# A residual block of a diffusion network on one core: every engine's instruction order written anew

## The chip, the cores and the metric

The kernel runs on one core of one Trainium2 chip, alone. The metric is the device time of one execution in microseconds, as the median of several runs. A profiled execution has a time of its own, and its span (from the first to the last recorded instruction) is a little shorter than that time.

## What is computed

The reference is the residual block of a diffusion UNet: group norm and SiLU, a 3x3 convolution, an embedding added per channel, group norm and SiLU again, a second 3x3 convolution, and the input added. B is 2, there are 512 channels, images of 64 x 64, four groups, and an embedding of 1152 numbers; everything is bfloat16 in and out.

```python
def gn(z, gamma, beta):                       # 4 groups of 128 channels
    mu = zr.mean(-1); var = ((zr - mu) ** 2).mean(-1)
    return (zr - mu) / jnp.sqrt(var + 1e-5) * gamma + beta
h = conv3(_silu(gn(x, g1, be1)), w1)          # 3x3, padding 1
h = h + (_silu(t_emb) @ w_emb).reshape(B, C, 1, 1)
h = conv3(_silu(gn(h, g2, be2)), w2)
return x + h
```

## The kernel before

**Tiling.** The channels are four tiles of 128, `ct` on the input side and `ot` on the output side. A *chunk* is 32 rows of one image (`b`, `ch`), so each of the two layers has four chunks, and each chunk four *groups*, one for each `ot`. A group is written here as layer.chunk.ot (g0.3.2 is the first layer's last chunk, third output tile). The convolution is done on rows in Winograd's way: each four rows of output come from six transformed planes `pos` 0 to 5. Planes 1 and 2 (in some chunks 1 to 4) are transformed along the columns too and called nested.

**The work of a chunk.** `produce_V` makes the transformed activations V of one chunk, tile by tile: SP loads the rows (line 619), ACT applies scale, bias and SiLU (`activate`, L626), and `transform` makes the planes on DVE (a scaled copy at line 641, then L642, L649, L662 to L679, then the columns at L557 and L562). Line 611 and 613 are POOL's memsets of the padding rows. Two V buffers stand in turn. `prep_U` makes the transformed weights U of half a tile (`pr`): loads of R and `g1t` by SP (the latter at line 404), scaled copies (lines 422 to 426), a sum by a DMA that accumulates, issued by POOL (L431), the combinations on DVE (L420), and `nest_U` (L393) for the nested planes. In layer 0, U of the later tiles is made during the first groups; U1.0p0 means layer 1, tile 0, first half. There are three `stage` buffers for the loads.

**The work of a group.** PE multiplies: nested planes with 256 columns (tile `nst`, L943), the others with 512 (tiles `mid` and `acc`, L935). PSUM has three buffers of two banks (`nst`, `mid` and an `aux` for sums) and two of one bank (`acc`). ACT copies the results out (`evac`, L306), DVE combines columns (`cols_mid`, L988 to L990, tiles `tu` and `rm`) and rows (`rows_z`, L1002 to L1009), and the two `acc` tiles of planes 0 and 5 are copied out in `close_group` while the next group is already under way. A POOL DMA adds z to y (L1070), SP stores to `h_scr` (L1074), and ACT takes the sums for the next norm (`sum_up`, L796). `tu` and `rm` have one buffer each.

**The norms.** `gn_scale_bias` takes the sums over the partitions by a matmul (L317) and then, on DVE, the negative variance (L319 to L330). POOL raises it to the power -1/2, for one column (L332) or four (L337), and DVE makes the scale `sc_all` (L333 or L338) and the bias `nb_all` from it. The first image's norm of layer 0 is done tile by tile (four powers of one column); the second image's, gn1, and the two of layer 1, gn2, in one power each.

**Who does a copy.** All scaled copies go through `scaled_copy`, which counts them; character k of the string `FLIP` moves copy k from its engine of default (DVE for `times`, ACT for `evac`) to the other. A copy on DVE is line L307, one on ACT L306.

**What sets the order.** `ORDER` is a table for each of five engine queues (PE, DVE, Activation, Pool, SP): the instructions of that engine by their number as written, in the order in which they are to be issued. `in_order` chains each to the one ahead of it:

```python
for a, z in zip(ranks, ranks[1:]):
    tc.add_manual_dep(mine[z], mine[a].name, info, reason="order")
```

The dependency only sets the order and adds no semaphore. The tables cover 3239 instructions of PE, 853 of DVE, 367 of ACT, 115 of POOL and 103 of SP. Waits between engines follow from the data and the buffers, as always. A planner has worked out the tables and the string from estimated durations of each kind of instruction and delays between engines.

Of the kernel before, what the change touches and what calls it, by code (L numbers as in the profile page):

```python
# [18 lines left out]
class _Background:  # L19
# [45 lines left out]
0-22 90-121 23-43 122 44-53 123-124 156-157 125-135 158-160 136-153 161-187 154-155 54-78 188-252 254-255 79-89 253  # L65
256-270 320-335 271-285 318 286-298 336-351 299-317 370-401 352 358 353 359-360 408-409 319 410 364 361-363 411-413
420 365 354-355 366-367 356-357 402-407 421-435 368-369 414-417 436-437 418-419 438-451 470-485 461 458-460 462
452-453 463 486-501 464-469 454-457 511-512 508-510 502-503 513-514 504-505 515 506-507 516 520-521 517-519 522-532
544 533-534 545 535 546-548 536 549-551 537 552-557 592 558-566 568-569 580 570 581 571-573 582-583 574 567 538-543
593 575-579 594-598 584-591 599-614 624-630 615-623 631-646 648 647 673-693 649-659 705 661-664 660 665 706 666-672  # L70
707-721 737-741 722-726 749 694-704 742-743 750 727-728 751-754 729-736 761-762 777 744-748 778 755-760 763 793-801
779 802-816 780-792 825-831 837-840 764-776 841-848 832-836 817-824 849-854 865-866 855-856 867-869 857 870-879 881
880 882-893 913 894-898 858-864 899-901 925-927 902-904 914-923 928-930 905 931 906-912 937-938 932-933 939-952 924
953 934-936 954-955 969-970 956-958 971 993 959-962 972-973 963-968 974-979 1001 994 980-985 1025-1026 986-992
1013-1014 1027-1028 1002-1003 1015 995-1000 1029-1032 1016-1022 1033 1023-1024 1041 1057 1004 1042-1043 1034-1040
1044 1005-1007 1058-1064 1008-1009 1045-1048 1081 1010-1012 1082 1065-1066 1083 1067-1070 1085-1086 1084 1049-1056
1097-1098 1071-1080 1099-1100 1109 1101-1102 1110 1103-1108 1087-1091 1111-1124 1092-1096 1125 1141 1126-1129 1142
1130-1140 1143-1147 1157-1172 1148-1156 1173-1178 1185-1190 1179-1180 1191-1192 1181 1193 1182 1194-1196 1183-1184
1197 1213-1214 1198-1200 1215-1216 1201-1204 1217-1219 1205-1212 1220-1232 1245-1260 1233-1244 1261-1262 1273-1274
1263-1271 1275-1281 1272 1282-1288 1301 1289 1302-1307 1290-1300 1308-1321 1333-1345 1322-1323 1346-1348 1324-1331  # L80
1349-1352 1332 1353 1361 1373-1375 1389-1390 1376-1378 1391-1394 1379-1386 1354 1395-1400 1355-1356 1387-1388
1401-1402 1362 1403-1405 1357 1363-1370 1358 1371 1359 1372 1360 1406-1412 1421 1413 1422-1427 1437 1428-1430 1438
1431-1435 1414-1416 1436 1417 1439 1418-1420 1450 1440-1442 1451-1452 1443-1446 1462 1447-1449 1453-1461 1478-1484
1463-1469 1494 1485-1490 1470-1473 1495 1491-1493 1496-1497 1474-1477 1498-1508 1526-1530 1510-1523 1509 1524-1525
1538-1542 1531-1535 1550 1566-1567 1536-1537 1543 1568 1544 1569-1570 1551-1554 1545-1548 1555-1557 1571 1558 1549
1559 1572-1580 1560-1565 1581-1597 1614-1616 1626 1617-1618 1627-1636 1598-1609 1637-1639 1610-1613 1640-1645
1619-1625 1646-1656 1670 1657 1671-1672 1658 1673-1679 1659-1661 1680-1685 1662-1669 1686-1698 1726-1730 1699-1701
1731 1702-1706 1714 1707-1710 1715-1725 1711 1732 1712-1713 1733-1740 1742-1743 1741 1758-1759 1744 1760 1745-1749
1761 1750-1757 1762-1773 1790-1793 1802 1774-1785 1794 1786-1789 1795 1803-1804 1796 1805-1806 1797-1798 1814
1807-1810 1799 1811-1813 1800-1801 1830-1837 1846-1847 1838-1839 1848-1854 1840-1843 1855-1857 1844-1845 1815-1818  # L90
1858-1859 1819 1860-1869 1820-1829 1870-1873 1882-1888 1894-1898 1889 1899-1900 1890-1893 1910 1901-1908 1874 1911
1926-1927 1909 1912 1928 1913-1916 1929 1875 1917-1922 1876 1923 1877 1924 1930-1931 1925 1878-1879 1932 1880-1881
1933-1949 1974-1979 1950 1980 1951-1955 1990-1992 1956-1957 1962 1958-1961 1963-1973 2006-2009 1981 2010-2015 1982
1993 2016-2018 1994-2003 2019-2021 2030 2022 2042-2043 2004-2005 1983-1987 2023-2028 2044 2031-2032 2029 2045-2048
1988-1989 2049 2033-2034 2050-2052 2054 2070 2086-2089 2055 2035 2090 2036 2071-2072 2037-2038 2053 2091 2056-2065
2092-2093 2066-2067 2039 2094 2068 2073 2040 2074 2095 2069 2075 2096 2041 2097-2102 2110 2103-2104 2111 2105-2108
2112 2123 2076 2124 2077-2080 2125 2081-2085 2126-2127 2113-2114 2128 2115-2117 2109 2118-2120 2129 2121-2122
2130-2131 2135-2143 2151 2144 2152-2153 2132-2133 2145-2146 2167 2147 2134 2154-2157 2148-2150 2158-2166 2168-2171
2183 2172-2182 2184-2197 2223-2224 2198 2225-2238 2199-2200 2211-2212 2201-2202 2239 2213 2240 2203 2255 2204-2205
2256-2257 2206-2209 2258-2260 2210 2214-2218 2241 2219 2242 2220-2222 2243-2250 2261-2262 2287 2251-2254 2263-2265  # L100
2299 2288-2293 2266-2269 2294-2295 2270-2285 2311-2314 2296 2286 2297-2298 2315-2325 2327-2331 2326 2332-2338
2343-2347 2339 2348-2349 2340 2350 2341-2342 2351-2358 2300-2310 2359-2367 2375 2368-2374 2376-2380 2399-2401 2387
2381 2402-2405 2382-2384 2406 2385 2388-2392 2415-2420 2393-2396 2421 2386 2422-2423 2407-2414 2424 2397 2425-2429
2431 2398 2430 2432-2438 2463-2465 2439-2462 2466-2468 2475-2476 2487 2477-2480 2488 2481-2482 2489 2483-2486 2503
2469-2474 2519-2534 2504-2508 2490-2502 2509-2518 2551-2556 2535-2550 2563 2557-2559 2564 2575 2565-2566 2576-2578
2567 2560-2561 2591 2568-2569 2579-2580 2592-2593 2581-2582 2607 2594 2608 2583 2609 2595 2584-2585 2596 2610-2613
2597-2601 2562 2614 2602 2615 2603-2604 2616 2605-2606 2617-2622 2570-2574 2586-2590 2639-2648 2651-2652 2649
2623-2638 2653-2656 2663-2671 2679 2672 2657 2673-2674 2650 2675-2677 2658 2678 2695-2705 2680-2694 2659-2662
2706-2726 2751-2756 2727-2728 2757-2758 2729-2731 2759 2739-2745 2760-2761 2746-2747 2762-2766 2748-2749 2767-2769
2750 2770-2773 2732-2734 2774-2781 2735-2738 2782-2793 2799-2811 2815-2820 2827-2829 2812-2814 2794-2798 2830-2831  # L110
2821-2822 2832-2834 2839 2823-2826 2835-2838 2840-2841 2855-2859 2842 2860-2862 2843 2863 2844-2854 2864-2866 2871
2867-2870 2872-2898 2935 2903-2905 2899-2902 2936-2949 2906-2910 2950 2911-2913 2951-2955 2919 2956-2962 2920 2963
2921 2967-2968 2922 2914-2918 2923 2969 2924-2925 2970-2971 2926 2964-2965 2972-2975 2966 2976-2978 2927 2979
2928-2929 2980-2982 2930-2931 2983-2985 2999-3000 2932-2934 3001-3005 2986-2998 3007 3006 3008-3014 3031-3039 3047
3040 3048 3041-3045 3049-3051 3046 3052-3055 3063-3064 3056-3057 3065 3058-3061 3015-3030 3066-3067 3062 3068-3069
3079 3070-3071 3080-3088 3072 3089-3093 3073 3094 3074-3075 3095 3159 3167 3096 3076-3078 3160 3097 3168 3161 3169
3162 3170-3173 3163-3166 3174 3098 3111-3112 3099-3104 3127 3113 3175 3183-3184 3114 3128 3115-3117 3129 3118-3119
3130 3105-3110 3131 3120-3123 3185-3186 3132 3124-3126 3187-3189 3133 3190 3143-3158 3134-3142 3176-3182 3191-3194
3215-3221 3195-3201 3222-3225 3202-3214 3226-3238""",
# [3 lines left out]
99 108 110 68 76 109 69 91 70 100 123 78 83 88 119 89 84 93 101 117 75 96 116 77 97 94 98 95 122 115 133 114 102 121  # L123
103 124 120 104 136 105 111 106 112 107 125 142 135 134 128 126 143 127 130 137 131 138 132 139 141 140 129 145 144
# [61 lines left out]
def kernel(  # L186
# [115 lines left out]
    def scaled_copy(o, i, f, on_act):  # L302
        k = n_copies[0]
        n_copies[0] += 1
        if on_act != (FLIP[k:k + 1] == "1"):
            return nc.scalar.activation(out=o, in_=i, func=ACT.Copy, scale=f)  # L306
# [921 lines left out]
```

## Time and profile before

| | before |
|---|---|
| runs (us) | 459.91, 460.68, 461.85 |
| median (us) | 460.68 |
| profiled execution: its time (us) | 461.23 |
| its span (us) | 459.1 |
| outside the span (us) | 2.1 |
| mean granted TensorE clock | 0.995 |
| PE, DVE, ACT, POOL busy (us) | 443.0, 435.6, 375.1, 76.4 |

A busy time counts each instruction from its start to its end; as consecutive ones overlap a little in the pipelines, the time from start to start is shorter. The first matmul starts at 1.4 us and the last ends at 453.6. In the table of slices the granted clock is below 9 tenths in one slice, around 234 us.

### The profile page before, as it was taken

How to read it: one execution, taken by the hardware profiler on the slowest of the kernel's cores; microseconds unless marked ns; L12 is line 12 of the kernel's file. 1: busy time of each engine (PE TensorE's matmuls, PEld its weight loads, DVE VectorE, ACT ScalarE, POOL GpSimd, SP SyncE). 2: the span in 40 equal slices, each digit the busy share in tenths (PEclk: the TensorE clock that was granted, in tenths of full speed). 3: DMA queues.
4: the chain of work that ended last, by engine and by line, in shares of the span. 5: the costliest groups of instructions: out<-in, count | busy, mean ns of one | idle time of the engine just before them, and what ended most of it. 6: DMA issues, size and time to landing. Idle time of an engine off the chain costs nothing.

```text
span 459.1 us, 8457 instructions
## 1 busy us (share of the span) xinstructions
PE 443.0 (96%) x3246; PEld 290.3 (63%) x3246; DVE 435.6 (95%) x857; ACT 375.1 (82%) x405; POOL 76.4 (17%) x119
## 2 busy tenths in 40 slices
PE   8988999999999999998989999999999999999995
PEld 7944455555555677666656555557676667668884
DVE  2999999989999999999999999999999899999986
ACT  5899997968967899889989999648686775869972
POOL 1231200041000000110211211124212121212110
PEclk9999999999999999999989999999999999999999
DMA  8998755544765463446889796375858769456673
GB/s 309 357 380 202 190 137 135 165 131 130 183 153 157 95 178 92 129 110 208 171 243 241 192 233 140 94 178 119 199 154 195 175 158 213 98 132 138 130 197 134
DMA packets 25010, 80.04 MB, mean 174 GB/s; under 512 B 2827, under 2 KB 6027, under 8 KB 24587
## 3 DMA queue, kind: packets, MB, share of 16 engines
q0 software_dynamic: 10080, 34.87, 37.2%
q1 hardware_dynamic: 14832, 44.64, 29.2%
q8 instruction: 25, 0.41, 0.3%
q14 instruction: 14, 0.11, 0.1%
q10 hardware_dynamic: 59, 0.01, 0.0%
HBM read 42.54 MB, written 16.78 MB: 129 GB/s over the span
## 4 chain that ended last, share of the span: by engine, by line
PE 48%; DVE 37%; issue 6%; ACT 4%; DMA 2%; POOL 2%; DVEq 0%; ACTq 0%; POOLq 0%
PE nst L943 22%; PE acc L935 18%; PE mid L935 6%; DVE V L679 4%; DVE ak L642 3%; DVE U L420 3%; DVE V L562 3%; DVE V L557 3%; DVE rm L990 2%; DVE U L393 2%; DVE ak L307 2%; DVE ak L649 2%; DVE V L669 1%; DVE tu L988 1%; DMA ak<-h_scr 1%
## 5 line engine op out<-in xcount | busy, mean ns | idle before, releaser
L943 PE MATMUL nst<-V,U 128*128 128x256 f16 x1600 | 205.3, 273 | 3.2 <-ACT rm L306 2.7
L943 PEld LDWEIGHTS <-U 128*128 128x128 f16 x1600 | 154.4, 97 | 50.3 <-issue 4.3
L935 PE MATMUL acc<-V,R 128*128 128x512 f16 x672 | 172.3, 384 | 3.1 <-ACT ring L306 1.7
L306 ACT ACTIVATE rm<-nst 128x1024 f16<-128x1024 f32 x98 | 98.1, 1024 | 23.4 <-PE nst L943 10.9
L935 PEld LDWEIGHTS <-R 128*128 128x128 bf16 x720 | 69.7, 97 | 68.4 <-issue 4.7
L935 PE MATMUL mid<-V,U 128*128 128x512 f16 x336 | 84.7, 384 | 1.6 <-DVE me L375 1.0
L626 ACT ACTIVATE ak<-ak,nb_all,sc_all 128x2112 f16<-128x2112 f16 (+1 forms) x28 | 59.8, 2148 | 4.6 <-DVE nb_all L525 1.9
L796 ACT ACTIVATE ring<-ring 128x2048 f16<-128x2048 f16 x32 | 61.3, 1914 | 1.4 <-ACT rm L306 0.7
L935 PEld LDWEIGHTS <-U 128*128 128x128 f16 x336 | 32.1, 97 | 36.1 <-ACT s_sb L450 1.1
L1070 POOL DMA_DIRECT2D ring<-ring x28 | 24.4, 872 | 148.0 <-ACT ring L306 131.4
L306 ACT ACTIVATE ring<-ring 128x512 f16<-128x512 f16 x47 | 27.8, 623 | 18.8 <-DVE ring L1002 10.5
L642 DVE TENSOR_TENSOR ak<-ak 128x2080 f16<-128x2080 f16 x32 | 40.0, 1249 | 0.8 <-ACT ak L306 0.6
L306 ACT ACTIVATE ak<-ak 128x520 f16<-128x520 f16 (+1 forms) x26 | 32.1, 1239 | 8.9 <-DVE ak L649 5.6
L679 DVE TENSOR_TENSOR V<-ak 128x1040 f16<-128x1040 f16 x54 | 39.0, 724 | 0.0
L562 DVE TENSOR_TENSOR V<-V 128x512 f16<-128x512 f16 (+1 forms) x62 | 35.2, 576 | 0.5 <-PE acc L935 0.5
L990 DVE TENSOR_TENSOR rm<-tu,rm 128x1024 f16<-128x1024 f16 x50 | 34.9, 698 | 0.9 <-DVE tu L988 0.5
L306 ACT ACTIVATE ring<-acc 128x512 f16<-128x512 f32 x55 | 31.3, 594 | 4.0 <-DVE ring L1009 3.1
L557 DVE TENSOR_TENSOR V<-V 128x1024 f16<-128x1024 f16 (+1 forms) x31 | 30.8, 996 | 0.0
L420 DVE TENSOR_TENSOR U<-U,g1t 128x1536 f16<-128x1536 f16 x32 | 30.6, 963 | 0.0
L989 DVE TENSOR_TENSOR tu<-rm 128x512 f16<-128x512 f16 x50 | 21.5, 431 | 1.6 <-ACT rm L306 1.6
L649 DVE TENSOR_TENSOR ak<-ak 128x1040 f16<-128x1040 f16 x32 | 23.0, 718 | 0.1
L669 DVE TENSOR_TENSOR V<-ak 128x1040 f16<-128x1040 f16 x32 | 22.9, 717 | 0.0
(131 smaller groups left out, 468.5 us busy)
## 6 DMA issues: line engine op xcount, KB each, us to landing
ring<-ring POOLq DMA_DIRECT2D x28, 512.0 KB, 4.7
ak<-h_scr SPq DMA_DIRECT2D x16, 528.0 KB, 5.4
h_scr<-ring SPq DMA_DIRECT2D x16, 512.0 KB, 3.7
ring<-in_x_dram POOLq DMA_DIRECT2D x14, 512.0 KB, 5.6
out_dram<-ring POOLq DMA_DIRECT2D x14, 512.0 KB, 5.2
ak<-in_x_dram SPq DMA_DIRECT2D x12, 528.0 KB, 4.9
R<-in_w_dram SPq DMA_DIRECT2D x16, 384.0 KB, 5.5
U<-U POOLq DMA_DIRECT2D x14, 384.0 KB, 5.3
```

Source lines behind the costliest of these rows:

```text
L306: return nc.scalar.activation(out=o, in_=i, func=ACT.Copy, scale=f)
L420: nc.vector.tensor_tensor(out=o, in0=i0, in1=i1, op=op)
L557: nc.vector.tensor_tensor(out=lo2.rearrange("p c q (t w) -> p (q t) c w", w=HALF), in0=plane_pair(0, HALF + 2), in1=plane_pair(1, HALF), o ...
L562: nc.vector.tensor_tensor(out=hi2[:, c].rearrange("p q (t w) -> p (q t) w", w=HALF), in0=i0, in1=i1, op=op)
L626: nc.scalar.activation(out=at[:, lo - r0:hi - r0, 1:W + 1], in_=sap, func=ACT.Silu, bias=nb_all[:, layer, b, ct:ct + 1], scale=sc_all[:, l ...
L642: nc.vector.tensor_tensor(out=diff, in0=diff, in1=below, op=ALU.add)
L649: nc.vector.tensor_tensor(out=rows(1, 2), in0=rows(1, 2), in1=rows(3, 2), op=ALU.subtract)
L679: nc.vector.tensor_tensor(out=o, in0=in0, in1=in1, op=op)
L796: behind(nc.scalar.activation(out=junk, in_=y, func=func, scale=scale, accum_out=acc), inst)
L935: nc.tensor.matmul(out, lhsT=w_direct(pos, ct, kx), rhs=rhs, start=first, stop=last)
L943: nc.tensor.matmul(accs["nst", (pos - 1) // 2][bank][:, q, :, plane, :], lhsT=lhsT, rhs=rhs.rearrange("p (t w) -> p t w", w=HALF), start=s ...
L990: nc.vector.tensor_tensor(out=msl[:, 1 - k:4 - k:2].rearrange("p q t w -> p q (t w)"), in0=tu[:].rearrange("p q t e w -> p q (t e w)"), in ...
```

## The change

All five tables of `ORDER` and the string `FLIP` are replaced; nothing else. The computation, the tiles, the buffers, the matmuls and the transfers are the same 4677 instructions in the tables. As told with the change, the new order was planned with longer times for GpSimd's powers (L332, L337) and for the weights' sums by transfers (L431), and with redrawn delays.

Of the 412 scaled copies 90 change engine: 50 go from DVE to ACT and 40 from ACT to DVE, so that DVE has 843 instructions and ACT 377. As an instruction's number in its table counts only the instructions of its engine, the numbers of DVE's and ACT's tables before and after don't denote the same instructions; PE's, POOL's and SP's do. Cut to the start of DVE's table, the small tables of POOL and SP, and the string:

```diff
@@ -62,110 +62,109 @@
 ORDER = {
...
     "DVE": """
-0 2 1 3-4 13-14 5 7 6 48 8 16 9 15 10 17 11 19 12 18 24-25 21 26 20 27 22 28 23 29-32 45 33 46 49 52 47 53 72 34 56
-35 50 38 54 71 36 55 37 39 57 51 40 58 41 74 113 42 73 80 85 43 81 44 87 86 79 59 82 60 92 61 90 62-64 66 65 118 67
...
     "Pool": """
-0 4 1 10-11 5 2-3 6-7 12-13 8-9 15 14 21-22 18 16-17 19 24 20 25 23 28 27 30 26 29 32-33 31 37 34 39 35 40 36 42 38
-41 47 43-45 49 46 50 48 64 52-53 65 55 51 56 54 68 57 69 59 58 60 62 61 63 66 81 67 70-73 78 74 83 75-77 86 79-80 82
-91 84-85 95 87-90 92 99 93 102 94 96-98 100-101 103-114""",
+0 4 1 10 5 11 2-3 6-7 12-13 8-9 21 14-15 22 16-17 20 18-19 25 24 23 28 27 30 26 29 32-33 31 37 34 39 35 40 36 42 38
+41 47 43 45 44 49 46 50 52 48 64 53 65 51 56 55 54 68 57 69 58-59 62 61 60 63 66 81 67 70-72 78 73-76 83 77 86 79-80
+82 91 84-85 95 87-90 92 99 93 102 94 96-98 100-101 103-114""",
     "SP": """
-0-13 17 19 21 18 20 23 14-15 22 16 25 28 30 33 24 26 29 31 27 32 37 35-36 34 39 38 40 42 44 43 41 45 48 50 47 46 49
-51 54 68 71 73 56 52 57 53 59 55 61 58 63 60 62 65 67 66 70 64 72 75 86-87 76-78 80 69 81-82 74 84 83 85 79 88-102""",
+0-13 17-19 21 23 20 14 22 15-16 25 28 30 33 24 26 29 31 27 32 37 35-36 34 39 38 40 42 44 43 41 45 48 50 46 49 47 54
+51 68 71 56 73 52 57 53 59 55 61 58 63 60 67 62 65 70 66 64 76 72 86 75 87 78 77 69 80 82 74 84 81 83 79 85 88-100
+102 101""",
 }
...
@@ -224,7 +223,7 @@
-    FLIP = "001011001000001100000000010000111000000010001111011111110000000001010001011000000001000000000001000000000000000000000000001000000000000000000000001101100000000000000000001000000010011110000000000001000000000000000001010000100000101001010001000010110111100100001101111100000111000000110010000100011001100000001110000001100000000010001001000011000000110011100000011111000000110000011000011100001100001110000111"
+    FLIP = "000110000000010000010000101000010101001110001001011111010000000011111000001111100001111100000100111001000000000101100000000001000001000000000000000101101000000010000000001010000000001011001000000001000000100000000010000101001000111001110010000011010111110100001101101100000011010000110110000110011111000000111010000001100000010010101001000110110000110011100000011111000000011000011000011100001100001000000111"
```

Read out, this is a stretch of DVE's queue around gn1, the second image's norm of layer 0 (V0.1 ct3 is the fourth tile of chunk 1 of layer 0; the number after a colon is the line):

```
before                          after
gn1 var           L330          gn1 var           L330
g0.0.3 cols_mid   L990          g0.0.3 cols_mid   L989
V0.1 ct3          L669          V0.1 ct3          L679
V0.1 ct3          L562          V0.1 ct3          L669
g0.0.3 rows_z     L1002         g0.0.3 cols_mid   L990
V0.1 ct3          L562          gn1 scale         L338
g0.0.3 rows_z     L1004         V0.1 ct3          L562, L562
gn1 scale         L338          gn1 bias          L339
nest_U            L393          nest_U            L393
g0.0.3 rows_z     L1008, L1009  g0.0.3 rows_z     L1002, L1004, L1006
gn1 bias          L339          gn1 bias          L340
nest_U            L393          V0.1 ct3          L557
gn1 bias          L340          g0.0.3 rows_z     L1009
nest_U            L393          g0.0.3 close_group, two copies
V0.1 ct3          L557          nest_U            L393
g0.1.0 cols_mid   L988, L989    g0.1.0 evac_nested, one copy
V0.2 ct0          L641, L642    nest_U            L393
...                             V0.2 ct0          L641
```

On POOL the sums of U0.2 and U0.3 (L431) go ahead of the first group's addition of z (L1070), the sum of U1.0p0 ahead of that of g0.3.0, and two memsets (L611, for V1.0 ct0 and V1.2 ct0) ahead of the powers of gn2. On SP the load of `g1t` for U1.1p1 (line 404) goes ahead of the load of R for U1.1p0 and of the rows for V1.1 ct0. PE's table has its groups in the same sequence; within and between neighbours, steps of different planes, groups and norms are interleaved differently.

More of the change, by code (lines that the diff above doesn't have):

```diff
@@ L70 @@
[L70 to L74, printed above, removed]
@@ L157 @@
[L157 to L161 removed]
+0-30 90-105 31-34 106-122 35-56 123 57-60 124 156-157 125-132 158-161 133-134 162-174 135-155 175-187 61-72 188
@@ new lines @@
+1002-1003 985-992 1015 1004-1009 1016-1019 993 1025 994-997 1020 998-1000 1021-1022 1010-1012 1041-1043 1026-1040
+1023-1024 1044-1048 1057-1059 1049-1052 1060-1062 1053-1056 1063-1082 1109-1112 1085 1113 1083-1084 1114-1119
+1097-1106 1120 1107-1108 1121-1123 1086-1096 1124-1147 1157-1172 1148-1156 1173-1182 1185-1196 1183-1184 1197-1238
+1245-1260 1239-1244 1261 1273 1262-1263 1274-1275 1264-1266 1276-1277 1267 1278-1280 1268-1269 1281 1270 1282
+1271-1272 1283 1285-1301 1284 1302-1354 1373-1383 1355 1384-1385 1356 1389-1390 1386-1388 1391-1396 1361 1397-1404
@@ new lines @@
+1362-1372 1357-1360 1405-1416 1421-1428 1437 1429-1436 1417-1420 1438-1441 1450 1442-1446 1451-1453 1447-1449
+1454-1460 1462 1478 1463 1461 1479-1481 1464-1467 1494 1468-1477 1482-1492 1526-1529 1493 1530-1531 1538-1543
+1510-1525 1495-1509 1532-1534 1544-1546 1535 1547 1536-1537 1548-1560 1566-1572 1561-1565 1573-1597 1614-1616
+1626-1628 1617 1598-1613 1638-1646 1618 1629 1619-1625 1647-1653 1630-1635 1654-1658 1670 1659 1636 1660-1669 1637
+1671-1701 1726-1727 1702 1728-1730 1703-1704 1714-1715 1705-1708 1716 1709-1710 1731 1711 1732-1736 1717-1723
@@ new lines @@
+1712-1713 1724-1725 1737-1744 1758-1759 1745 1760-1765 1746-1747 1766 1748-1757 1767-1773 1790-1792 1802-1803
+1774-1789 1804 1793-1794 1805-1811 1795 1812-1813 1796-1801 1814-1816 1830-1838 1846-1848 1839-1845 1849-1866
+1817-1829 1867-1874 1882-1883 1894-1895 1910 1896-1901 1926-1927 1884-1887 1928 1888-1889 1902-1903 1890 1911 1875
+1912 1876-1877 1929 1878-1879 1930-1933 1904 1934-1938 1905 1880 1913-1918 1881 1919-1923 1906 1891-1893 1924-1925
+1907-1909 1939-1948 1950-1951 1949 1952-1971 1974-1976 1972-1973 1977-1979 1990 2006 1991 2007-2008 1980 2009
@@ new lines @@
+1992-2003 2010-2019 2004-2005 1981-1989 2030-2032 2020-2024 2042-2050 2054-2057 2051-2053 2058-2062 2070 2063-2064
+2071-2073 2025-2026 2033 2027-2029 2034-2039 2086-2089 2074 2090-2093 2075-2077 2040 2065 2078-2081 2066 2082-2084
+2094-2096 2085 2097-2100 2067-2069 2101-2103 2041 2104-2108 2110 2109 2111 2123 2112 2124-2126 2135 2127-2131
+2136-2137 2132 2138-2144 2113-2114 2133 2115-2116 2151-2157 2145 2158-2159 2146 2160-2164 2147-2150 2117 2165-2166
+2118-2122 2167 2134 2168-2173 2183-2198 2174-2182 2199-2201 2223-2226 2211 2202 2212-2213 2203 2214-2215 2239-2243
@@ new lines @@
+2216-2217 2204-2206 2244-2247 2207 2248-2252 2208-2210 2227-2237 2218 2238 2219 2253-2254 2220-2222 2255-2269 2287
+2270 2288-2289 2271-2286 2290 2299 2291-2293 2311-2321 2294-2295 2322 2296 2300 2297-2298 2301-2309 2327-2330
+2323-2324 2331-2333 2325-2326 2334 2343-2344 2335-2342 2310 2345-2354 2359-2374 2355-2358 2399-2405 2375-2378 2387
+2379-2385 2406 2388-2390 2415-2417 2407-2412 2431-2434 2413 2386 2414 2391-2393 2418-2430 2394-2396 2435-2436 2397
+2437-2438 2398 2439-2445 2463-2464 2447-2448 2446 2449-2462 2465-2469 2475-2476 2470-2472 2477-2478 2487 2473
@@ new lines @@
+2935-2939 2903-2905 2911-2912 2940-2943 2906-2909 2944 2910 2945-2948 2913 2949 2914-2915 2950 2916-2917 2951 2918
+2967 2952-2955 2968-2970 2919-2926 2971 2956-2959 2972-2973 2960-2964 2974-2976 2965-2966 2977-2978 2927-2929
+2999-3000 2930-2934 3001-3004 2983-2998 3005 2979 3031-3033 2980-2982 3034-3041 3006 3042-3044 3007 3045 3008-3009
+3047 3010-3014 3048-3052 3063 3053 3015 3054-3059 3016 3060 3023-3030 3017-3018 3064-3066 3046 3067-3068 3061-3062
+3069-3076 3019-3022 3077-3095 3159-3163 3167-3168 3164-3166 3096-3097 3169-3174 3098-3104 3175 3105-3109 3111
@@ new lines @@
+3127-3128 3112-3117 3183-3187 3118 3110 3188-3190 3119-3126 3129 3143-3158 3130-3142 3176-3182 3191-3198 3215
+3199-3200 3216 3201 3217-3238 3202-3214""",
+    "DVE": """
+0-2 4 3 13 5 7 14-16 6 50 8-10 17 20 19 11 18 26 25 22 27 12 28 21 29 23-24 30 46 31-32 47 33 48 51 34 49 35 52 54
+36 55 75 40 56 39 37 53 38 113 58 57 41 74 59 84 60 42 117 61 43 62 88 63 44 77 83 45 82 64 114 87 65 102 67 66 68
+93 79 69 71 70 112 72 89 73 92 116 118 85 81 76 115 90 86 94 123 91 109 122 124 119 97 95 125 121 98-99 103 101 100
@@ new lines @@
+721 717 713 722 719-720 723 729-730 711 731 724-726 735 734 727 736 728 737-738 732 739 733 740-742 746-747 743 748
+744-745 749-751 761 758-759 752-753 757 767 756 768 754-755 771 770 760 764 772 769 762 765 763 766 774 773 775 777
+776 779 782 780 784 783 778 781 789-790 785 791 786-787 792-793 788 794 796 795 800 798 801-802 799 804 803 797 808
+807 805 809 806 810-812 814 813 819 816 815 818 817 820-821 836 835 822-827 837 829 828 838 831 830 832-833 841 834
+842 839-840""",
+    "Activation": """
@@ L162 @@
+336-337 330-331 334-335 339 338 346 342 347 343-344 341 348 340 349 345 360 351 350 355 359 356 352 354 353 358
+361-362 357 364 363 373-374 365-366 376 367 369 368 375 370 372 371""",
     "Pool": """
[L163 to L165 removed]
+0 4 1 10 5 11 2-3 6-7 12-13 8-9 21 14-15 22 16-17 20 18-19 25 24 23 28 27 30 26 29 32-33 31 37 34 39 35 40 36 42 38
```

138 lines of the change are left out of this document (50 added, 88 removed).

## The prediction

> **What bounds the kernel now.** I read the page first, then stretches of the span, then who waits for whom, then single rows around the places where TensorE stops. From the page:
>
> ```profile
> span 459.1 us, 8457 instructions
> ...
> PE 443.0 (96%) x3246; PEld 290.3 (63%) x3246; DVE 435.6 (95%) x857; ACT 375.1 (82%) x405; POOL 76.4 (17%) x119
> ...
> PE 48%; DVE 37%; issue 6%; ACT 4%; DMA 2%; POOL 2%; DVEq 0%; ACTq 0%; POOLq 0%
> ```
>
> Two engines are full and share the chain. An order can therefore only win back idle time of PE, or of DVE where PE waits for it. To find that time I summed, from the trace's rows, each engine's work from start to start; an engine's *lag* at an instruction is its start minus all its own work ahead of it. PE's work is 435.1 us (nst 0.109 us each, the 512-wide ones 0.222), so its lag ends at 18.3. It grows like this: 10.4 at 45 us, 11.4 at 120, 11.5 at 203, 13.9 at 219, 16.2 at 232, 17.87 at 240, then almost flat. The idle time to be won in the steady stretches is 1 us between 45 and 203 and 0.4 us after 240. The rest is start-up (10.4) and the layer change (6.4). The stretches show it (columns: us, then PE, PEld, DVE, ACT, POOL busy, granted clock, DMA share, GB/s):
>
> ```profile
> 80.00:120.00 40.00, 39.36 (x239) 21.24 (x238) 38.09 (x75) 33.65 (x35) 7.04 (x7) 1.00 0.54 157
> 120.00:160.00 40.00, 40.00 (x255) 23.61 (x254) 40.00 (x76) 32.33 (x33) 3.23 (x7) 1.00 0.53 137
> ...
> 216.00:220.00 4.00, 2.53 (x16) 1.36 (x15) 4.00 (x8) 4.00 (x6) 0.84 (x2) 1.00 0.34 135
> 230.00:234.00 4.00, 1.87 (x14) 1.37 (x12) 4.00 (x9) 3.29 (x5) 0.00 (x0) 0.88 0.84 298
> 234.00:238.00 4.00, 4.00 (x23) 2.69 (x22) 3.17 (x6) 2.93 (x5) 1.75 (x2) 0.69 0.80 202
> ```
>
> At 216.6 PE stands still for 1.64 us, at 230.5 for 2.29 us, and from 233.1 the clock column falls: for 3.41 us a nested matmul takes 0.213 us, which costs 1.68 us. The waits (engine, line, waited for: us in total, times, longest):
>
> ```profile
> ACT rm L306 <- DVE rm L990: 5.0, 4, 3.6
> DVE sc_all L338 <- POOL var L337: 2.8, 3, 0.9
> PE nst L943 <- ACT rm L306: 2.7, 2, 2.1
> DVE ak L307 <- ACT ak L626: 1.9, 2, 1.0
> DVE sc_all L333 <- POOL var L332: 1.3, 3, 0.5
> ```
>
> The two rows on sc_all are DVE waiting for GpSimd's powers, 4.1 us together; the first and third are the stall at 230 (PE waits for ACT's evacuation, which waited for DVE). No DVE row names the weights' sums by transfers (L431): the use, L420, follows without a gap everywhere.
>
> **The powers.** On POOL's and then DVE's timeline, one power of four columns and one of a single column:
>
> ```profile
> 24.87 0.88 POOL L332 TENSOR_TENSOR var<-var,neg_half 128x1 f32<-128x1 f32 x1 [2.08 <-DVE var L330]
> ...
> 93.60 3.92 POOL L337 TENSOR_TENSOR var<-var,neg_half 128x4 f32<-128x4 f32 x1 [6.84 <-DVE var L330]
> ```
> ```profile
> 24.57 0.15 DVE L330 TENSOR_SCALAR var<-var 128x1 f32<-128x1 f32 x1
> ...
> 25.26 0.15 DVE L375 TENSOR_SCALAR me<-ga 128x1 f32<-128x1 f32 x1
> ...
> 26.01 0.16 DVE L333 TENSOR_TENSOR sc_all<-var,gb 128x1 f32<-128x1 f32 x1
> ...
> 93.34 0.18 DVE L330 TENSOR_SCALAR var<-var 128x4 f32<-128x4 f32 x1
> ...
> 95.91 0.70 DVE L1004 TENSOR_TENSOR ring<-rm 128x1024 f16<-128x1024 f16 x1
> 97.56 0.16 DVE L338 TENSOR_TENSOR sc_all<-var,gb 128x4 f32<-128x4 f32 x1 [0.94 <-POOL var L337]
> ```
>
> The seven powers have 0.87, 0.87, 1.38, 0.81, 3.11, 1.22 and 1.82 us of DVE work between var and use. Those of one column last 1.27, 1.26, 0.88 and 1.07 us and DVE waits 0.46, 0.44, 0 and 0.44; those of four last 3.92, 2.02 and 2.62 us and DVE waits 0.94, 0.93 and 0.93. The power ends a fixed time after DVE's work has run out, however much work lay between; the one without a wait (24.87) is the one with a small PSUM-reading op (L375) in the middle. So this power does not run beside DVE's large two-input copies: it waits for them. The new order puts 1.41, 1.74, 2.11, 2.04, 2.18, 1.27 and 1.80 us between, of the same large kinds save for the third. By these rows every wait stays and its result comes later by the added work: worth 0 on DVE. Had the powers simply run from var on, 0.9 to 1.3 us of a single-column one would be covered, and up to 4.1 us would go; I take 0, the rows' own pattern, and keep 4.1 for the range. [...]
>
> **The weights' sums.** Fourteen DMAs, 0.87 us of POOL each, landing after 5.3 us (median). They already land in time, so giving them longer buys 0. The price of moving them: on POOL those of U0.2 and U0.3 go ahead of the first group's z addition (L1070), and two memsets (L611) ahead of gn2's powers, 0.2 us each and ready earlier; POOL is 17% busy; 0. On SP one g1 load (L404) goes ahead of the R load and the V1.1 ct0 load. It waits for a stage buffer that comes free near 225.3 by the new DVE order; landing at 230.6 (5.3 us), it reaches ACT's copy ahead of g0.3.2's evacuation with nothing to spare: 0, up to 1 us.
>
> **The copies that change engine.** 90 of 412 scaled copies: 50 go from DVE to ACT, 40 back. With the rows' start-to-start times (DVE/ACT: 2080 wide 0.61/1.83, 1536 0.47/1.37, 520 0.21/0.53, 512 from SBUF 0.20/0.52, 512 from PSUM 0.60/0.48), DVE loses 16.6 us and gains 15.4 (431.6 to 430.4); ACT gains 42.7 and loses 28.4 (362.7 to 376.9). ACT's extra falls at 80 to 160 (11.3 us: 66 of 80 us busy become 77) and at 320 to 400 (6.0).
>
> **The order itself.** I compared, for each group, the work ahead of the same step in both queues. On DVE, rows_z of the groups from 45 to 200 us stand 0.6 to 3.2 us later, gn2's use (195.87) 1.7 us later; from the second layer's fifth group on everything is about 1 us earlier. PE's order hardly changes its own work. The wait at 102.73 (0.91 us, DVE for ACT's L626) goes: 4.7 us of DVE work now lie between nb_all and the copy, against 2.04 for the activation. PE is 100% busy there, so I take 0 of PE's time for it; it pays back part of DVE's lateness.
>
> The layer change, followed through: gn2's scale at 195.87 + 1.69 - 0.91 = 196.65; V1.0 ct0 on ACT at 197.85 (was 197.35); ACT's work from there to g0.3.2's evacuation 33.1 us (32.6), so 230.95 at the earliest, where before it began at 231.88 after waiting for DVE. The stall at 216.6 shrinks from 1.64 to about 1.35, that at 230.5 from 2.29 to 1.5; a new one near 235, for close_group of g0.3.1, costs 1.2. Before: 1.64 + 2.29 + 1.68 (clock) = 5.61; after: 1.35 + 1.5 + 1.2 = 4.05; gain 1.56 if the clock stays up. From below, PE's lag after the change is at least DVE's (13.3 to 14.3 here) plus 2.69 + 0.15 of work from DVE's last step to PE's first in g1.0.0: 16.1 to 17.1 against 17.87, a gain between 1.7 and 0.8. I take 0.8, since DVE enters this stretch late rather than early.
>
> A 2.29 us stop halved the clock here, one of 1.64 did not. [...]
>
> After 240: V1.2's ct0 copy now runs on ACT, so DVE waits up to 1.8 us near 320, while PE has 0.6 us to spare by lag (16.4 against 17.0): 0, up to 1.2. The tail after the last matmul (5.5 us) loses 0.4 us of DVE copies and gains as much on ACT: 0.
>
> **Sum**, against the profiled execution's 461.23 us (span 459.1 and 2.1 around it): start 0, powers 0, weights 0, 45 to 203 us 0, layer change -0.8, rest 0: 460.4. That execution lies 0.55 above the median of the runs, so the median becomes 459.9. About 0.5% (2.3 us) is what a measurement here can tell from no change: faster is below 458.4, slower above 463.0.
>
> **Rivals.**
> *Faster.* The powers do get covered: DVE gains the five waits ahead of the layer change (0.46 + 0.44 + 0.44 + 0.94 + 0.93 = 3.2), enters it that much earlier, and PE's stop at 230 goes with its slow clock, less the new wait: 2.29 + 1.68 - 1.2 = 2.8; 461.23 - 2.8 - 0.55 = 457.9, and with 0.6 us from the start-up's PE gaps (8.0 us of them in the first 40) 457.3. For: the waits are real. Against: the rows above.
> *Slower: ACT becomes the late engine.* Each of the nine 2080-wide copies that go to ACT holds it 1.83 us. PE's three two-bank PSUM buffers give it 0.05 to 0.9 us of slack before an evacuation between 45 and 203 (from the rows). An evacuation behind such a copy comes up to 1.83 late: 0.93 lost beyond the slack; if half of the nine hit, 4.2 us. Place: 80 to 160, where ACT goes to 97%. It decides once evacuations wait over 0.9 us. 461.23 + 4.2 - 0.55 = 464.9. For: rows_z stands 0.6 to 3.2 us later on DVE as well. Against: by queue sums PE's lag bound there is 11.1 against 11.4 now, and DVE lightens in the same places.
> *Nothing changes.* The order does not act where it aims, the stall at 230 stays over some 2 us and the clock falls again (1.68): 461.23 + 0.3 - 0.55 = 461.0.
>
> **Numbers.** Forecast 0.36 (459.9), faster rival 0.25 (457.3), slower 0.28 (464.9), nothing 0.11 (461.0). Faster: 0.25 and 0.02 of the forecast's spread; slower: 0.28 and 0.03; same 0.42. The range takes in the faster rival with 0.8 of spread (456.5) and the slower one with 0.6 (465.5).
>
> **What would show it.** Right: L338 still with 0.9 us of wait; powers longer where more work lies between; no wait at L307 near 103; PE's stalls near 217 and 230 under 2 us and the clock column at 1.00 in all slices; no PE gaps over 0.5 us from 120 to 200. Wrong: PE rows below 40.00 in the 40-us stretches from 80 to 200 with ACT's rm as releaser, or PE's lag at 240 outside 16 to 18.3.

## The result, and the profile after

The new order is slower: 463.75 us median (461.89 to 465.96) against 460.30 (459.28 to 461.85) for the kernel before in the same runs, a ratio of 1.0075 with a 95% interval of 1.0057 to 1.0092. That is 3.45 us, where 0.8 less was forecast. The profiled execution of the new kernel is one of its slowest (465.96 us, 2.2 above its median), so the terms read from it come out larger than the medians'. One line of the kernel is gone, so its line numbers are one lower than before: L1001 was L1002, L795 was L796.

The page of the new kernel:

```profile
span 463.9 us, 8487 instructions
...
PE 443.8 (96%) x3246; PEld 290.0 (63%) x3246; DVE 435.9 (94%) x847; ACT 385.8 (83%) x415; POOL 75.9 (16%) x119
...
PE 29%; DVE 24%; issue 9%; ACT 6%; DMA 5%; POOL 1%; DVEq 0%; ACTq 0%; POOLq 0%
```

PE and DVE do the same work as before, and ACT 10.7 us more. What is new in the chain is the share of DMA, 5% instead of 2%: work now waits for transfers. The stretches (us; PE, PEld, DVE, ACT, POOL busy; granted clock, DMA share, GB/s):

```profile
60.00:80.00 20.00, 18.01 (x99) 9.82 (x97) 18.45 (x30) 15.27 (x19) 1.19 (x3) 0.91 0.51 124
80.00:120.00 40.00, 40.00 (x239) 21.23 (x238) 38.10 (x75) 36.33 (x38) 6.26 (x8) 1.00 0.50 146
120.00:160.00 40.00, 38.47 (x250) 23.13 (x249) 38.17 (x70) 35.06 (x36) 2.21 (x5) 1.00 0.51 138
160.00:200.00 40.00, 38.11 (x270) 25.75 (x269) 38.20 (x77) 34.45 (x37) 3.31 (x6) 1.00 0.45 124
230.00:234.00 4.00, 4.00 (x32) 2.83 (x30) 4.00 (x7) 3.97 (x5) 0.15 (x1) 1.00 0.78 217
236.00:240.00 4.00, 1.75 (x17) 1.47 (x16) 4.00 (x9) 4.00 (x6) 0.00 (x0) 1.00 0.49 192
```

Before, PE was full from 120 to 200. Now it stops once in each of three stretches (here and below a stop is named by the time of its end): at 72.2 for 1.90 us, followed by a half clock (granted 0.50 from 73 to 76 us) that costs 0.09 x 20 = 1.8 us; at 157.2 for 1.53; at 196.9 for 1.89. In the same stretches DVE and ACT are idle too (DVE 18.45 of 20, 38.17 and 38.20 of 40 us busy). PE's lag, before and after, is 10.4 and 10.2 at 60 us, 10.4 and 14.1 at 80, 11.4 and 15.7 at 160, 11.5 and 18.0 at 203, 17.9 and 21.7 at 240, 18.3 and 22.8 at 452. So the loss lies between 60 and 203. The layer change looks 2.7 us shorter; that it isn't is shown below. The waits of the new kernel:

```profile
ACT ring L795 <- DMA ring<-ring: 7.9, 3, 3.1
PE nst L942 <- ACT rm L305: 6.0, 4, 2.2
PEld aux L316 <- ACT rm L305: 2.5, 2, 2.3
DVE sc_all L337 <- POOL var L336: 0.9, 1, 0.9
```

The first line was 0.4 us in the kernel before:

```profile
ACT ring L796 <- DMA ring<-ring: 0.4, 2, 0.2
```

L795 is `sum_up`: ACT's sums over a finished output tile, which need z's transfer (L1069) to have landed. ACT's timeline around the first two of the three waits:

```profile
64.50 1.91 ACT L795 ACTIVATE ring<-ring 128x2048 f16<-128x2048 f16 x1 [2.80 <-DMA ring<-ring]
67.15 1.89 ACT L795 ACTIVATE ring<-ring 128x2048 f16<-128x2048 f16 x1
71.12 1.00 ACT L305 ACTIVATE rm<-nst 128x1024 f16<-128x1024 f32 x1
...
150.15 1.91 ACT L795 ACTIVATE ring<-ring 128x2048 f16<-128x2048 f16 x1 [3.13 <-DMA ring<-ring]
152.19 1.91 ACT L795 ACTIVATE ring<-ring 128x2048 f16<-128x2048 f16 x1
154.10 2.14 ACT L625 ACTIVATE ak<-ak,nb_all,sc_all 128x2112 f16<-128x2112 bf16 x1
156.13 1.00 ACT L305 ACTIVATE rm<-nst 128x1024 f16<-128x1024 f32 x1
```

The evacuations (rm<-nst) that PE waits for stand behind the sums. An order that queues the three pairs of sums behind the copies that PE waits for deadlocks, so there is no time for it. That the two cannot simply change places can be seen on DVE's timeline:

```profile
154.22 0.69 DVE L1001 TENSOR_TENSOR ring<-rm 128x1024 f16<-128x1024 f16 x1 [1.63 <-ACT ring L795]
```

The next group's `rows_z` waits for the second sum (152.19 + 1.91 = 154.10). It reads rm, of which there is one buffer, so the next evacuation waits for `rows_z`. In the code both write into `ring`: `rows_z` with one access pattern from a slot of y to a slot of z, the sums a by-product into the slot between them. The chain is: z's transfer lands, two sums (3.9 us), `rows_z`, the evacuation, PE. Other work in ACT's queue lengthens it: at the first stop four copies stand between the second sum and the evacuation (69.04 to 71.12), at the second the activation L625 (2.14 us), which holds the evacuation until 156.13, though this `rows_z` step, the last to read rm, had ended at 154.91.

Why the first one lands late, from the DMA issues between 50 and 70 us (KB each, us to landing):

```profile
U<-U POOLq DMA_DIRECT2D x2, 384.0 KB, 5.4
ring<-ring POOLq DMA_DIRECT2D x1, 512.0 KB, 8.8
```

Two weights' sums were issued in POOL's queue just ahead of it (from 52.7 on, z at 55.65), and it took 8.8 us; before it took 4.4 (issued at 54.75). The other two landed after 7.0 and 7.4 us, each beside an activation load of 528 KB that SP issued within 0.8 us of it (142.95 and 183.93).

### The profile page after: what moved, and what is told of

Same layout as the page of the kernel before. It is cut to its first block, busy times and chain, and to the rows that moved or that the text cites. A ratio compares the mean times of both kernels' runs of the same rounds, so it can differ in the third digit from the quotient of the medians.

```text
span 463.9 us, 8487 instructions
## 1 busy us (share of the span) xinstructions
PE 443.8 (96%) x3246; PEld 290.0 (63%) x3246; DVE 435.9 (94%) x847; ACT 385.8 (83%) x415; POOL 75.9 (16%) x119
## 4 chain that ended last, share of the span: by engine, by line
PE 29%; DVE 24%; issue 9%; ACT 6%; DMA 5%; POOL 1%; DVEq 0%; ACTq 0%; POOLq 0%
PE nst L942 17%; PE acc L934 9%; DMA ring<-ring 4%; PE acc L1037 2%; DVE V L678 2%; DVE rm L989 2%; DVE ak L641 2%; ACT ring L795 2%; ACT rm L305 2%; DMA out_dram<-ring 1%; DVE U L419 1%; DVE ak L648 1%; DVE ring L1003 1%; DVE ring L1001 1%; DVE V L556 1%
## 5 line engine op out<-in xcount | busy, mean ns | idle before, releaser
L305 ACT ACTIVATE rm<-nst 128x1024 f16<-128x1024 f32 x97 | 97.0, 1027 | 14.8 <-PE nst L942 6.5
L795 ACT ACTIVATE ring<-ring 128x2048 f16<-128x2048 f16 x32 | 61.4, 1918 | 8.0 <-DMA ring<-ring 7.9
L625 ACT ACTIVATE ak<-ak,nb_all,sc_all 128x2112 f16<-128x2112 f16 (+1 forms) x28 | 60.1, 2150 | 3.2 <-DVE V L561 1.1
L1069 POOL DMA_DIRECT2D ring<-ring x28 | 24.6, 880 | 159.6 <-ACT ring L305 136.1
L305 ACT ACTIVATE ak<-ak 128x520 f16<-128x520 f16 (+1 forms) x38 | 46.4, 1228 | 5.1 <-DVE ak L648 2.7
L305 ACT ACTIVATE ring<-ring 128x512 f16<-128x512 f16 x49 | 29.6, 625 | 22.2 <-DVE ring L1001 14.6
L678 DVE TENSOR_TENSOR V<-ak 128x1040 f16<-128x1040 f16 x54 | 38.2, 708 | 0.1
L561 DVE TENSOR_TENSOR V<-V 128x512 f16<-128x512 f16 (+1 forms) x62 | 33.9, 558 | 0.0
L305 ACT ACTIVATE ring<-acc 128x512 f16<-128x512 f32 x48 | 27.1, 594 | 2.0 <-issue 1.1
L668 DVE TENSOR_TENSOR V<-ak 128x1040 f16<-128x1040 f16 x32 | 22.4, 699 | 0.0
```

What stands on the lines that cost most here:

```text
L561: nc.vector.tensor_tensor(out=hi2[:, c].rearrange("p q (t w) -> p (q t) w", w=HALF), in0=i0, in1=i1, op=op)
L625: nc.scalar.activation(out=at[:, lo - r0:hi - r0, 1:W + 1], in_=sap, func=ACT.Silu, bias=nb_all[:, layer, b, ct:ct + 1], scale=sc_all[:, l ...
L678: nc.vector.tensor_tensor(out=o, in0=in0, in1=in1, op=op)
L795: behind(nc.scalar.activation(out=junk, in_=y, func=func, scale=scale, accum_out=acc), inst)
```

## The experiments

Each kernel ran on the same chip as the kernel before (460.4 to 460.8 us median there). The tables are numbers, so the edits are given in the queues' words.

**Where the loss sits.** Two kernels join the orders at the layer change, with the engine of each copy taken along.

```diff
 every queue: what the kernel before had started by 205 us, in its order
-then the rest in the order before
+then the rest in the new order
```

> All that the kernel before had started by 205 us in its own order and with its own copies, then the rest in the new order with the new choice of engines. It has none of the three late sums. Theory A (the new order's loss lies wholly in the first layer, its layer change is better by itself): PE's lag rises by 3.7 us or less over 203 to 240 instead of 6.4, 457 to 459 us. Theory C (the new layer change only looked short because PE came to it 6.5 us late while the rest was ready): lag rises by 6 to 7 us again, 460 to 461.5 us.

Measured: 460.30 us, ratio 0.9997 (0.9985 to 1.0009). PE stops for 1.94 us at 219 and 1.66 at 233, the clock stays up, and the lag rises by 4.0 over the layer change. The time is theory C's. The lag is neither's, and nearer to A's 3.7 than to C's 6 to 7: of the 6.4 us in the kernel before, 1.7 were the half clock, which did not come here. The new order's second half is worth nothing that can be measured.

```diff
 every queue: what the new kernel had started by 209 us, in its order
-then the rest in the new order
+then the rest in the order before
```

> All that the new kernel had started by 209 us in its own order, then the rest in the order of the kernel before. It keeps the three late sums. Theory A (loss in the first layer, and the old layer change loses its full 6.4 us on top of the lag of 18.0): 464 to 467 us. Theory C (the layer change is set by DVE's lateness, so a late PE loses little there): 462 to 464 us.

Measured: 464.03 us, 1.0074 (1.0055 to 1.0093): the whole loss, from the first layer alone. The value lies at the lower edge of what A expected and at the upper edge of C. In its profile the stops at 154 (1.53) and 194 (1.46) are there; the first is only 0.40, at 70.5, without a half clock, in the very same order. There z's transfer took 7.3 us instead of 8.8. This profiled execution is the fastest of its kernel (462.07 us), while that of the new kernel was its slowest.

**Whether z's transfer is the cause.** The transfer made short, in both orders:

```diff
+ZN = CR * W // 4 if layer == 0 else CR * W
-out=flat(yst), in_=ring[:, NY + turn % NZ], accum_op=ALU.add)
+out=flat(yst)[:, 0:ZN], in_=ring[:, NY + turn % NZ, 0:ZN], accum_op=ALU.add)
```

> The new kernel in which the transfer that adds z to y carries only a quarter of the columns in the first layer (the other three quarters of z are left out of y; everything else is issued as before). Theory A (the first layer's loss is the chain: z's transfer lands, then two sums on ACT, then rows_z on DVE, which waits for the sums, then the next evacuation, then PE): the transfer lands in 2 to 3.5 us instead of 4.4 to 8.8, ACT's 7.9 us of waiting for it fall under 1.5, PE's stops near 72, 157 and 197 fall under 0.6 us each; 458.5 to 461 us. Theory B (ACT is too full, the transfer is only what its queue happens to wait for): the stops stay above 1 us, 462.5 to 464.5 us.

> The kernel before with the same edit: z's transfers of the first layer carry a quarter of the columns. It is the control. Theory A: this order hardly waits for the transfers (ACT 0.4 us in all, PE 1 us between 45 and 203), so 459.5 to 461 us, under 1 us from its own time. If it falls as far as the new kernel does (2 us or more), the smaller traffic itself is the gain and theory A is not shown.

Measured: the new order 459.20 us, 0.9969 (0.9956 to 0.9981); the old one 460.49, 0.9994 (0.9983 to 1.0005). The same edit takes 4.5 us from the one and nothing that can be measured from the other. With short transfers the new order is even 1.3 us faster than the old one; by PE's lag this comes from its start-up (see below). The new order with short transfers, its landings, waits and stretches:

```profile
ring<-ring POOLq DMA_DIRECT2D x16, 128.0 KB, 2.7
```
```profile
ACT ring L795 <- DMA ring<-ring: 1.0, 2, 0.8
```
```profile
60.00:80.00 20.00, 19.90 (x115) 10.91 (x114) 20.00 (x35) 17.14 (x21) 1.19 (x3) 1.00 0.42 109
120.00:160.00 40.00, 40.00 (x254) 23.50 (x253) 39.97 (x72) 37.35 (x37) 3.24 (x7) 1.00 0.39 106
160.00:200.00 40.00, 40.00 (x295) 28.03 (x293) 39.65 (x87) 34.73 (x37) 4.42 (x7) 1.00 0.31 91
```

All three stops are gone, while ACT has the same instructions and is 93% busy from 120 to 160 (37.35 of 40 us, against 35.06 with the full transfers). This settles theory A against B. Whether a late landing would have cost as much with the old choice of engines is open: no run moves the 90 copies alone.

**The queue of POOL's transfers.** z first, as in the kernel before:

```diff
 POOL, new order
+z addition of g0.0.0
 weights' sum U0.3, second half
 weights' sum U0.3, first half
-z addition of g0.0.0
```

> The new kernel with one move on POOL: the z addition of g0.0.0 is issued ahead of the two weights' sums of U0.3, as in the kernel before; the rest is the new order. Theory A (the transfer lands late, 8.8 us after its issue, because two weights' sums of 384 KB stand ahead of it in its queue): it lands in 4.5 to 5.5 us, the sum on ACT starts by 62 instead of 64.5, PE's stop at 72.2 and the half clock behind it go, the other two stops stay: 3 to 3.7 us less in the first layer, 460 to 462.5 us at the end. Theory B (order in the queue does not matter, other transfers slow it): 463 to 464.5 us.

Measured: 470.19 us, 1.0206 (1.0187 to 1.0225). Neither expectation holds. z does land early: the first sum starts at 61.76 without a wait. But now the weights are late, on DVE's timeline:

```profile
67.26 0.96 DVE L419 TENSOR_TENSOR U<-U,g1t 128x1536 f16<-128x1536 f16 x1 [5.80 <-DMA U<-U]
```

DVE had put this use at 61.2. The sums are issued only after POOL has waited for z, 3.6 us later than in the new order, and land behind it after 8.4 and 10.3 us instead of 4.7 and 6.0. PE stops for 5.87 us at 76.3. What stood close behind another transfer in this queue landed late in these two orders: z after 8.8 us in the new one, the weights after 8.4 and 10.3 in this one.

```diff
 POOL, order before
-z addition of g0.0.0
 memset of padding rows (L613)
 weights' sum U0.3, second half
+z addition of g0.0.0
```

> The kernel before with one move on POOL, as in the new order: the weights' sum of U0.3, second half, is issued ahead of the z addition of g0.0.0. Theory A: issued right behind a transfer of 384 KB in the same queue, z's transfer takes 7 to 9 us instead of 4.4 and lands at 63.5 to 65; ACT's sum (62.80 before) waits 1 to 2 us, PE near 70 stops for up to 1 us: 460.5 to 462.5 us. If order in the queue costs nothing, it lands 4.4 to 5 us after its issue and the time is 460 to 461.

Measured: 460.96 us, 1.0005 (0.9987 to 1.0023). As expected, z's transfer takes 7.1 us instead of 4.4 and ACT waits. It is also issued later, at 57.95 instead of 54.75 in the kernel before and 55.81 in the run with z first, since it now stands behind the memset as well, which waits 5.60 us for DVE:

```profile
65.09 1.91 ACT L796 ACTIVATE ring<-ring 128x2048 f16<-128x2048 f16 x1 [0.90 <-DMA ring<-ring]
```

The wait of 0.9 us costs PE no stop over 0.35 us near 70. In this order the same exchange is nearly covered, in the new one, where two sums go ahead of z, it isn't.

**The order repaired.** One sum ahead of z, by the time of its use:

```diff
 POOL, new order
-weights' sum U0.3, second half (used at 67.3)
 weights' sum U0.3, first half (used at 61.2)
 z addition of g0.0.0
+weights' sum U0.3, second half
 ACT
+copy of U0.3 (66.41)
 first sum (64.50)
-copy of U0.3 (66.41)
```

> The new kernel with POOL's order at the first z addition changed to: weights' sum U0.3 first half (DVE uses it at 61.2), z addition of g0.0.0, weights' sum U0.3 second half (used at 67.3); on ACT the copy of U0.3 (66.41) ahead of the first sum. Theory A: only one transfer stands ahead of z's, which lands by 61 to 62 instead of 62.8 to 64.5, the weights arrive before they are used (no DVE wait at L419 over 0.5 us), PE's stop near 72 falls under 0.5 us, those near 157 and 197 stay: 1 to 2 us less, 461.5 to 463 us. If DVE waits for U instead, as it did when z went ahead of both, 464 us and more.

Measured: 462.10 us, 1.0043 (1.0028 to 1.0059): 1.65 us less than the new order, and 1.66 above the kernel before on its own chip, where the new order was 3.45 above. z lands after 5.1 us, the stop near 72 is gone, those at 154.9 (1.52) and 194.5 (1.71) stay. Next, the loads behind z:

```diff
 SP, as well
-load of rows V0.3 ct1 (142.95)
 store of g0.1.2
+load of rows V0.3 ct1
-load of rows V1.0 ct0 (183.93)
 store of g0.2.1
+load of rows V1.0 ct0
 ACT: activation of V0.3 ct1 behind the next two evacuations
```

> The same, and the loads of 528 KB that share the transfer engines with two later z additions are issued behind them: on SP the load of V0.3 ct1 (142.95) goes behind the store of g0.1.2, the load of V1.0 ct0 (183.93) behind the store of g0.2.1, and ACT's activation of V0.3 ct1 behind the next two evacuations. Nothing is left out. Theory A: z's transfers of g0.1.2 and g0.2.1 land in 4.5 to 5 us instead of 7.0 and 7.4, all three stops in the first layer fall under 0.6 us, and the time comes near that of the run with a quarter of z: 459 to 460.5 us. If the landings stay at 7 us, the loads are not what slows them: 461.5 to 463 us.

Measured: 460.39 us, 0.9995 (0.9984 to 1.0007): another 1.7 us, and no loss that can be measured is left. The landings are 5.1, 4.7 and 6.1 us (the last above the 5 expected), the stops 0.64 us at 155 and 0.60 at 191. The edit moves an activation on ACT too. The stop goes without that move too: with short transfers the activation stands where it did, ACT's longest wait for z is the same 0.8 us, and PE is full from 120 to 160 (40.00 of 40 us). The stretches show that the repair is not whole, since PE was full in both before:

```profile
120.00:160.00 40.00, 39.36 (x249) 22.95 (x247) 38.53 (x69) 35.87 (x36) 3.22 (x7) 1.00 0.48 135
160.00:200.00 40.00, 39.12 (x279) 26.57 (x278) 39.27 (x86) 34.30 (x36) 4.26 (x7) 1.00 0.46 128
```

PE's lag rises by 3.2 us from 45 to 203, against 1.3 in the kernel before and 1.1 with short transfers. The time comes out level because of the new order's better start-up (below). These repairs move only a few entries; the copies' engines, the powers and the rest of the new order are left as they are.

```diff
 DVE: second large step of rows_z g0.3.1 ahead of V1.0 ct3 (L648) and V1.0 ct2 (L556)
 ACT: first evacuation of g0.3.2 ahead of the copies of V1.0 ct3 and U1.1
```

> The same as the last, and at the layer change two moves for the stop near 235: on DVE rows_z of g0.3.1 (the second of its two large steps) ahead of V1.0 ct3's and ct2's steps, and on ACT the first evacuation of g0.3.2 ahead of two copies (V1.0 ct3, U1.1). Theory A': the evacuation waits for rows_z, which reads the one rm buffer, so it starts 1.2 us earlier and PE's stop falls from 2.2 to about 1 us: 458 to 459.5 us. Rival: V1.0 ct3 comes a microsecond later and g1.0.0 waits for it instead: no change against the last, 459 to 460.5 us.

Measured: 460.30 us, 0.9998 (0.9987 to 1.0009). The stop falls from 2.23 to 1.28 us, as A' says, and a second one of 0.78 appears at 234. The time is the rival's; its mechanism is not, as the second stop waits for the next evacuation and not for V1.0 ct3. Then the second evacuation as well:

```diff
 ACT: second evacuation of g0.3.2 behind the first, ahead of three copies
```

> The last repaired order with one more move at the layer change: on ACT the second evacuation of g0.3.2 follows the first at once, ahead of the copies of V1.0 ct3, U1.1 and rows_z. Theory A' (PE's second stop there, 0.8 us, waits only for that evacuation's place in ACT's queue): the stop goes, 459 to 460 us. Rival (V1.0 ct3's copy comes 0.9 us later and DVE or g1.0.0 waits for it): no change, 460 to 460.7 us.

Measured: 460.75 us, 1.0007 (0.9996 to 1.0017). The time lies just above both expectations. The 0.78 us goes and 1.18 us appears 0.7 us later at an acc tile, whose own evacuation now comes later. No version with the full transfers beat the kernel before.

**The powers.**

```diff
 DVE, order before
-use of a power of one column (L333), three times
 one to two instructions that follow (L307 x1; L375, L370; L307 x1)
+use of that power
+rows_z g0.0.3 copy (L307, 512 columns)
 use of gn1's power (L338)
-rows_z g0.0.3 copy
```

> The kernel before with only DVE's order touched at the powers: in the first, second and fourth of one column the use (L333, L334) moves one to two instructions later (a one-input copy of 768, two small PSUM readers, a one-input copy of 768), and ahead of gn1's use (L338) stands one copy of 512 more (L307). Theory P (a power gets through at the end of the DVE instruction that it met, about 0.41 us later, and a one-input copy lets it through): the three waits of 0.44 to 0.46 go, gn1's wait falls from 0.94 to about 0.7; DVE's lag is 1.3 to 1.5 us lower from 31 us on. For the time: if DVE's waits at the powers are worth anything to PE, 459 to 460 us; if PE is not held by DVE there, no change, 460 to 461. If the powers are shut out by any DVE instruction, the waits stay at 0.44 and 0.94.

Measured: 460.48 us, 0.9995 (0.9985 to 1.0006). The waits fall from 1.3 to 0.6 us (one column) and gn1's from 0.94 to 0.61, theory P in part; the time does not move. Of the three waits two go or nearly go, to 0 and 0.19 us. The third, among one-input copies alone, stays at 0.44: there one more copy of 768 made the power longer, 1.34 us instead of 1.07 in the kernel before.

**The start-up alone.**

```diff
 every queue: what the new kernel had started by 45 us in its order,
 then the rest in the order before
```

> All that the new kernel had started by 45 us in its own order and on its own engines, the rest in the order of the kernel before. By the profiles the new start-up has PE's lag some 1 to 2 us lower at 45 us. If the steady stretch and the layer change carry that through: 458.5 to 459.8 us. If DVE's lag (10.2 against 10.8 at 45) is what counts at the layer change: 0.6 us less at most, 459.8 to 460.7 us.

Measured: 461.18 us, 1.0006 (0.9996 to 1.0016). The median lies above both expectations, and by the ratio nothing has changed: PE's lag, lower at 45 us, rises by 1.7 us up to 60, under the order before.

The lead itself stands in the profiles. With one price per shape of matmul, PE's lag at 45 us is 10.2 to 11.5 us (mean 11.0) in the five profiled executions that start in the old order, and 8.5 to 10.1 (mean 9.3) in the nine that start in the new one. With short transfers it is kept, and the new order is 1.3 us faster; with the full ones it is spent up to 203 us.

## Why the prediction was wrong, step by step

**The step that failed** is "45 to 203 us 0". The bound behind it compared queues of engines two by two and left out the leg through a transfer: evacuation, z's transfer, sums, `rows_z`, evacuation. In the kernel before, seven of the sixteen pairs of sums start 4.6 to 5.4 us after z's issue, against a landing of 4.8 us (their median), and four have idle time of 0.02 to 0.69 us in front of them, so there was little slack to give. By the profile the term is +6.7 us (3.9 near 72 with the half clock, 1.6 and 2.1 at the other two, less 0.9 for two old stops that went). In the faster execution with the first layer in the new order (462.07 us) the lag rises by 5.2 us from 45 to 203, 3.9 more than before. By the medians the whole change is 3.45, of which the repairs took back 1.65 and 1.7.

**The start** was put at 0 as well. The profiles give the new order some 1.7 us there, so the loss behind it is larger than the medians show: the two together make the 3.45.

**The moves on POOL** were put at 0 because POOL is 17% busy. Its issuing was free; the queue of its transfers was not: 8.8 us to landing instead of 4.4. On SP the prediction priced one weights' load only, which nothing waited for at the layer change, and not the two activation loads that met z's transfers.

**The weights' sums**: "giving them longer buys 0" holds, since no use waited before, but the price was what they displaced.

**The powers**: "every wait stays" was wrong. Of 4.1 us of DVE's waits 0.9 is left. The new kernel's timelines, POOL and DVE:

```profile
12.88 1.36 POOL L331 TENSOR_TENSOR var<-var,neg_half 128x1 f32<-128x1 f32 x1 [10.55 <-DVE var L329]
```
```profile
12.71 0.95 DVE L419 TENSOR_TENSOR U<-U,g1t 128x1536 f16<-128x1536 f16 x1
13.58 0.62 DVE L306 TENSOR_SCALAR U<-R 128x768 f16<-128x768 bf16 x2
14.27 0.16 DVE L332 TENSOR_TENSOR sc_all<-var,gb 128x1 f32<-128x1 f32 x1
```

The power ends at 14.24, beside two one-input copies, 0.58 us after the two-input step ended. The prediction counted such copies among the work that shuts it out; these two did not, though those beside the third wait of the run above did (0.44 us). What was right is the value: 0 for the time. The run with only the powers' uses moved shows that for the 1.0 us of waits that it takes away; gn2's powers were not moved alone. The rival "faster" had its mechanism come true and its price not.

**The layer change**: -0.8 rested on the half clock of 1.68 us in the profiled execution of before. It belongs to that execution, not to the order: in the controls with the old order there (short z, U first, powers) the lag rises by 4.2 us and the clock stays at 1.00, much as the 4.0 of the new one. In the repaired run and in the one with short transfers the half clock came in the new order's layer change (granted 0.79 over 8 us in each). The term was near 0. Of its parts, the stop expected at 1.35 measured 1.13; those of 1.5 and 1.2 came as a single one of 2.25.

**The rival "slower"** had the sign and nearly the size (464.9), with another mechanism: not the wide copies on ACT, as the short transfers show at the same ACT work, but what ACT was made to wait for. What stood for it in the prediction, `rows_z` 0.6 to 3.2 us later on DVE, may have been a sign of the true one, since z's transfer leaves behind `rows_z`; no run tests that.

## What to carry to other kernels

Follow a chain through its transfers too: put each DMA's landing, not its issue, into the order, and write down the slack in front of the first instruction that needs it. An engine with little to do is no proof that moving things in its queue is free: z's transfer landed after 4.4 us with no weights' sum close ahead (the last 5.5 us earlier), after 7.1 close behind one and after 7.3 to 8.8 behind two. The one that others wait for first should not stand second. A lead can also hide a loss, so compare the lag stretch by stretch and in more than one execution, not only the time at the end. Before a saving is credited for a slow clock, look whether it is there in other executions of the same order.

## What the runs showed of the hardware

**A half clock after some stops.** A stop of PE of some 2 us is followed by 3.4 us of half clock (granted 0.50) in some executions and not in others. The same stretch with a stop of 2.23 us (repaired order) and of 2.16 us (powers moved), granted clock third from the end:

```profile
230.00:238.00 8.00, 5.76 (x33) 3.56 (x31) 8.00 (x17) 7.38 (x9) 0.86 (x1) 0.79 0.62 190
```
```profile
230.00:238.00 8.00, 5.84 (x44) 4.03 (x42) 8.00 (x16) 7.07 (x12) 1.75 (x2) 1.00 0.83 261
```

0.21 x 8 = 1.7 us of difference. A stop of 1.90 us brought it (new order, 72.2), one of 2.62 us did not (new first layer, old rest, 235). The length of the stop alone does not tell; what does, no run shows.

**GpSimd's power beside DVE.** In the kernel before, the new one and the run with the powers moved, a power of four columns ended 0.9 us (0.89 to 0.91 in the first two) after DVE's two-input steps paused or gave way to a one-input copy. One of a single column ended 0.40 to 0.42 us after the end of a large two-input step in nine of twelve cases and 0.58 in one (12.88 above). The other two, among one-input copies alone, ended 0.40 and 0.42 us after the last of these. In the run with the powers moved the copy of 512 columns did not hold the power up: it ended at 98.42, 0.90 us after the two-input step ahead of the copy. Why one-input copies held a power up in those two cases and not here, the runs do not show.
